# Attention and two feed-forward networks on one core: mirrored tiles turned one pair ahead, stores issued later, a subtraction on another engine

## The chip, the cores and the metric

One core of a Trainium2 chip runs the whole program in one launch. The metric is the device time of the execution in microseconds, as the median of several runs; lower is better.

## The reference

An attention without softmax (batch 2, sequence 3008, model width 256, key width 64) feeds two feed-forward networks in a row. All inputs are float32; the weights of the networks arrive as float64 words, which the kernel turns into float32 itself.

```python
scores = (1/S) * z @ z.T          # z: (2, 3008, 64), S = 3008
attn   = maximum(scores, 0) ** 2
x      = u * (attn @ v)           # u, v: (2, 3008, 256); x as (6016, 256)
h = x @ w_in1;  x = (h - tanh(h)) @ w_out1            # d_ff = 2048
h = x @ w_in2;  g = h where h >= 1, 0 where h <= -1, else (h + 1)**2 / 4
out = g @ w_out2
```

## The kernel before

Every float32 operand of a matmul is split into a rounded part and a rest (`hi`, `lo`), and three products replace one. ScalarE makes `hi` (a copy or a square with rounding), VectorE makes `lo` by a subtraction.

**Attention.** For each of two batches `b` there are six rows `c` of 512 queries (448 in the last), and in each row twelve pairs `t` of 128-key tiles, 144 pairs in all. A loop over the pairs (`i`, L1089) emits, for each: loads (`pump`), `get`s of mirrored blocks, hooks, the first product of pair `i` (`first_product`), the second product (with V) of pair `i - 2` (`second`, LAG = 2), a slice of weight conversion (`make`), and last the functions in `tail` (`close`). Each engine works its queue in this order; waits are on semaphores.

The score matrix is symmetric. A block of rows `c` and columns `e` with `c < e` is computed in row `c`, squared into `ax` and stored by `put` (L292) in a DRAM tensor `mir`; in row `e` it is fetched by `get` (L309) as two tiles `m` (eight DMAs, issued some pairs ahead), and `mirrored` (L324) turns its 32x32 blocks on VectorE into `am` (L333, two transposes), rounds it on ScalarE (`hi`, L337) and puts the subtraction (`lo`, L339) into `tail`. 60 of the 144 pairs are mirrored: none in row 0, two more in each further row, ten of twelve in row 5, so there they stand one behind the other. A pair that is not mirrored runs six score matmuls (L353), then relu and squares (L378, L381, L384) and `lo` (L396).

The queries of rows 0 to 4 are read by the score matmuls in a permuted order of 32-element runs (`turned`, L284), so the accumulators are permuted, and the end of a row undoes it (`y`, L457 on ScalarE and L458 on VectorE, read from PSUM; the next row's accumulation needs those banks). For the mirrored tiles to come out in that same order, `put` permutes rows while it stores, with four DMAs a tile.

**The queue of SyncE.** Nearly every DMA is issued from SyncE in program order: loads of z, v, u (L131, L136, L163, L268), `put` (L300 to L305), `get` (L318), conversion loads and stores (L196, L245), the finished rows (L471). One that waits for its source holds back all behind it. `put` and the rows' stores stand in `deferred`, which is emptied (`flush`) within the next pair.

**Conversion.** `convert` (L192) turns sixteen pairs of weight tiles (1024 columns of `w_in`, 512 of `w_out` each) into float32 halves on VectorE, ends with sums on GpSimd (L232), the rounding on ScalarE (L236), and the subtraction on VectorE (L241), and stores them. `work` gives it VectorE time as a credit: 1.5 for each pair that is not mirrored in rows 1 to 5, 1.4 for each `fill` in the networks; every step is charged its stated cost, the subtraction 1.2 or 0.69.

**Networks.** After the attention 88 units of 42 matmuls and the last tile's own loop follow; weights are streamed from DRAM for each unit.

Of the kernel before, what the change touches and what calls it, by code (L numbers as in the profile page):

```python
# [7 lines left out]
F32 = mybir.dt.float32  # L8
# [7 lines left out]
P = 128  # L16
# [15 lines left out]
def attention_then_two_ffn(  # L32
# [57 lines left out]

    loads = []
    deferred = []

    def add_load(first, last, steps, slots=1):
        loads.append({"first": first, "last": last, "steps": steps, "slots": slots})
# [3 lines left out]
            fn()  # L99
        deferred.clear()  # L100

    def split(hi, lo, src, now=False, on_vector=False):
        if on_vector:
            nc.vector.tensor_copy(out=hi, in_=src)
        else:
            nc.scalar.activation(out=hi, in_=src, func=AF.Copy)

        def rest():
            nc.vector.tensor_tensor(out=lo, in0=src, in1=hi.bitcast(F32), op=ALU.subtract)

        if now:
            rest()
        else:
            deferred.append(rest)
# [40 lines left out]
    def load_v(b, t):  # L155

        st = {}

        def dma(queue=nc.sync):
            r = st["raw"] = raw_p.tile([P, 512], F32, tag="raw", name=f"vraw{b}_{t}")  # L160
            r3 = r.rearrange("p (t d) -> p t d", d=D)
            n = min(2, NFULL - 2 * t)
            queue.dma_start(  # L163
                out=r3[:, :n, :],
                in_=v[b, 2 * t * P : (2 * t + n) * P, :].rearrange("(t p) d -> p t d", p=P),
            )
            if n < 2:
                for h in range(2):
                    nc.sync.dma_start(out=r3[64 * h : 64 * h + 64, 1, :], in_=v[b, NFULL * P :, :])

        def work(on_vector=False):
            r = st["raw"]
            w = ring.tile([P, 2, 512], F32R, tag="w", name=f"v{b}_{t}")
            if 2 * t + 1 < NFULL:
                split(w[:, 0, :], w[:, 1, :], r, on_vector=on_vector)
            else:
                split(w[:, 0, :D], w[:, 1, :D], r[:, :D])
                nc.scalar.activation(out=w[0:64, 0, D:], in_=r[0:64, D:], func=AF.Copy)
                split(w[64:128, 1, D:], w[64:128, 0, D:], r[64:128, D:])
            vs[b, t] = w  # L180

        return [(dma, AHEAD), (work, 2)]
# [9 lines left out]
    def convert(net, f, which, src):  # L192
# [45 lines left out]
        def rest():  # L238
            hi = st["hi"]
            lo = prep_p.tile([P, 1024], F32R, tag="lo", name=f"pl{nm}")  # L240
            nc.vector.tensor_tensor(out=lo[:, :n], in0=w[:, :n], in1=hi[:, :n].bitcast(F32), op=ALU.subtract)  # L241
            to = packed[net, f]
            for i, part in enumerate((hi, lo)):
                out_ = to[:, i, :] if which == "in" else to[:, 2, i * 512 : i * 512 + 512]
                nc.sync.dma_start(out=out_, in_=part[:, :n].bitcast(F32))  # L245
            done.add((net, f, which))

        if which == "in":
            posts.append((0.0, sums))
        posts.append((0.0, rounded))  # L250
        posts.append((1.2 if which == "in" else 0.69, rest))
        yield 0.69


# [37 lines left out]
    def put(b, c, t, a):  # L292

        e, h = divmod(t, 2)
        to = mir[b, c, e]
        tiles = slice(2 * h, 2 * h + 2)
        if e < QC - 1:
            to = to.rearrange("t p q -> (t p) q").rearrange("(i t b) q -> i t b q", i=4, t=4)
            for i in range(4):
                nc.sync.dma_start(out=to[i, tiles].rearrange("t b q -> b t q"), in_=a[32 * i : 32 * i + 32])  # L300
        elif t < NPA - 1:
            nc.sync.dma_start(out=to[tiles].rearrange("t p q -> p t q"), in_=a)
        else:
            nc.sync.dma_start(out=to[2], in_=a[:, 0])
            nc.sync.dma_start(out=to[3, :REST], in_=a[:REST, 1])  # L305
# [15 lines left out]
                )  # L321
            got[b, c, e].append((m, k))

    def mirrored(b, c, t):  # L324

        n = min(QT, S - QT * c)
        e, h = divmod(t, 2)
        a = tmp_p.tile([P, 2, 512], F32, tag="t2", name="am")
        hi = sp_p.tile([P, 2, 512], F32R, tag="hi", name="hi")
        lo = sp_p.tile([P, 2, 512], F32R, tag="lo", name="lo")  # L330
        s = (slice(None), slice(None), slice(0, n))
        for part, (m, k) in enumerate(got[b, e, c]):
            nc.vector.transpose(  # L333
                out=a[:, :, 256 * part : 256 * part + 32 * k].rearrange("p t (k a) -> p t k a", a=32),
                in_=m[:, :k, 2 * h : 2 * h + 2].rearrange("p k t a -> p t k a"),
            )
        nc.scalar.activation(out=hi[s], in_=a[s], func=AF.Copy)  # L337
        flush()
        tail.append(lambda: nc.vector.tensor_tensor(out=lo[s], in0=a[s], in1=hi.bitcast(F32)[s], op=ALU.subtract))  # L339
        return hi, lo, n  # L340

    def attn_s(b, c, t):
# [49 lines left out]
            tail.append(square_hi) if late else square_hi()  # L392
        flush()
        if out_:
            deferred.append(lambda: put(b, c, t, a))
        tail.append(lambda: nc.vector.tensor_tensor(out=lo[s], in0=a[s], in1=hi.bitcast(F32)[s], op=ALU.subtract))  # L396
        return hi, lo, n

    def attn_av(b, c, t, hi, lo, n):
# [7 lines left out]
        def mm(d, j, part, g, start=False, stop=False):  # L407
            for h in range(2):
                half = slice(64 * h, 64 * h + 64)
                lhsT = w[half, part, j * D + d * P : j * D + (d + 1) * P]  # L410
                nc.tensor.matmul(acc[d][h][:, :n], lhsT, g[half, j, :n], start=start, stop=stop)  # L411

        def his(d):
            for j in range(2):
# [45 lines left out]
        def scaled():  # L460
# [7 lines left out]
            while o < n:  # L468
                g, r = divmod(b * S + QT * c + o, 2 * QT)
                k = min(n - o, 2 * QT - r)  # L470
                nc.sync.dma_start(out=kept[0, g][:, :, r : r + k], in_=ut[:, :, o : o + k])  # L471
                o += k

        deferred.append(scaled)
# [93 lines left out]
    def fill():  # L568

        if fills:  # L570
            for fn in fills.pop(0):
                if fn is not None:
                    fn()
        else:
            work(CONVERT[1])

    def copy(out_, in_):
        nc.scalar.activation(out=out_, in_=in_, func=AF.Copy)  # L578
# [49 lines left out]
    class Unit:  # L628
# [59 lines left out]
        def emit(self, p, att=None):  # L688
# [60 lines left out]
            self.A.value()  # L749
            if att:  # L750
                flush()
            add(self.B.h[:, 0, :w], u2, V[:, :w])
            for fn in three:
                fn()
# [225 lines left out]
    with tc.manual_schedule():  # L980
# [88 lines left out]
                fn()  # L1069
            tail.clear()  # L1070

        def first_product(i):
            if i < len(pairs):
                s_fn, _, args = pairs[i]
                held[i] = s_fn(*args)
            else:
                flush()

# [7 lines left out]
        for k in range(3):  # L1086
            hook(NATT - 3 + k, load_w, k)

        for i in range(NATT):  # L1089
            pump(i)  # L1090
            while blocks and i + 1 >= blocks[0][3] - LEAD and sum(x > i for x in reading) < READ:
                *block, _, last = blocks.pop(0)
# [3 lines left out]
                fn(*args)  # L1096
            if i == LAG:
                second(i)
            if not (LAG < i - 1 and at[pairs[i - 1 - LAG][2]] == 0):
                first_product(i)  # L1100
            if LAG < i and at[pairs[i - LAG][2]] == 0:
                first_product(i + 1)
            if i == 0:
                close()
                z1["steps"][2][0]()
# [6 lines left out]
                second(i)  # L1112
            make(i)
            close()

        ps_s_guard.__exit__(None, None, None)
        ps_f = ctx.enter_context(
# [79 lines left out]
```

## Time and profile before

| | |
|---|---|
| median of 3 runs | 1520.16 us (1520.08 to 1520.57) |
| the profiled execution | 1520.33 us, span 1518.5 us |
| TensorE (matmul) busy | 1456.2 us, 96% of the span |
| VectorE busy | 1250.9 us, 82% |
| ScalarE busy | 981.1 us, 65% |
| GpSimd busy | 46.5 us, 3% |

The attention takes the first 545 us or so, the networks the rest. Engine names in the rows: PE is TensorE's matmul, PEld its weight load, DVE VectorE, ACT ScalarE, POOL GpSimd, SPq the queue of SyncE; L337 is line 337 of the kernel. The text gives the granted clock as a share of the full 2.4 GHz.

### The profile page before, as it was taken

Reading aid. Unit: us, or ns where it says so; the run is one execution under the profiler, and the core shown is the slowest. Engines: PE = TensorE matmul, PEld = TensorE weight load, DVE = VectorE, ACT = ScalarE, POOL = GpSimd, SP = SyncE. Lnnn points to the kernel's source line nnn. Section 1 sums busy time; section 2 is a strip of 40 time slices with the busy share of each in tenths; the row PEclk is TensorE's granted clock in tenths of the full one; section 3 lists DMA queues with packets and bytes.
Section 4 is the critical chain, followed back from the end, with each engine's and each line's share of the span. In section 5 each row is a group of like instructions: output and inputs, shape, how many; then the busy total and the mean of one; then the engine's idle time right before and its main releaser. Section 6 shows DMA issues by size and latency. Waiting matters only on the chain.

```text
span 1518.5 us, 22103 instructions
## 1 busy us (share of the span) xinstructions
PE 1456.2 (96%) x8293; PEld 1196.1 (79%) x8293; DVE 1250.9 (82%) x1551; ACT 981.1 (65%) x1209; POOL 46.5 (3%) x69
## 2 busy tenths in 40 slices
PE   8899898999987899999999999999999999999998
PEld 6688677786765678888888888988887878888897
DVE  6788778777876778989898988888889898888775
ACT  6687643887754366676767766766666666666543
POOL 0100000000000000000000000000000000000000
PEclk9899999999999999999999999999999999999999
DMA  7698878489878654837475665656554545647361
GB/s 177 194 279 243 218 176 198 121 238 264 231 196 219 211 208 127 321 121 275 172 239 202 235 238 206 247 203 223 181 151 163 169 168 184 204 151 234 125 194 25
DMA packets 282652, 301.12 MB, mean 198 GB/s; under 512 B 136880, under 2 KB 204848, under 8 KB 282544
## 3 DMA queue, kind: packets, MB, share of 16 engines
q1 hardware_dynamic: 281344, 299.44, 63.5%
q8 instruction: 65, 1.06, 0.3%
q10 hardware_dynamic: 1200, 0.26, 0.1%
q14 instruction: 43, 0.35, 0.1%
HBM read 225.84 MB, written 73.79 MB: 197 GB/s over the span
## 4 chain that ended last, share of the span: by engine, by line
PE 65%; ACT 9%; DMA 8%; DVE 7%; SPq 7%; issue 4%; ACTq 0%; DVEq 0%; POOL 0%; POOLq 0%
PE acc L661 29%; PE m L642 25%; PE acc L411 5%; SPq L318 3%; DMA m<-mir 3%; PE h L830 3%; ACT r L378 2%; DVE am L333 2%; PE acc L866 1%; SPq L300 1%; ACT hi L337 1%; PE acc L887 1%; ACT ax L384 1%; SPq L268 1%; DMA wideout<-in_moe_w_out_dram 1%
## 5 line engine op out<-in xcount | busy, mean ns | idle before, releaser
L411 PE MATMUL acc<-hi,v 64*128 64x512 f32 (+1 forms) x2256 | 311.1, 401 | 47.5 <-ACT hi L337 21.0
L411 PEld LDWEIGHTS acc<-hi,v 64*128 64x128 f32 x2256 | 232.1, 191 | 104.9 <-ACT hi L337 34.1
L642 PE MATMUL m<-xht,w 128*128 128x512 f32 (+1 forms) x704 | 215.7, 388 | 0.0
L661 PE MATMUL acc<-ghb,w 128*128 128x512 f32 (+1 forms) x704 | 187.8, 388 | 0.0
L661 PE MATMUL acc<-gha,w 128*128 128x512 f32 (+1 forms) x704 | 173.4, 387 | 0.0
L411 PE MATMUL acc<-lo,v 64*128 64x512 f32 (+1 forms) x1104 | 165.5, 394 | 2.9 <-DVE lo L396 2.6
L337 ACT ACTIVATE hi<-am 128x1024 fp32r<-128x1024 f32 (+1 forms) x60 | 61.4, 1023 | 155.1 <-DVE am L333 136.9
L661 PEld LDWEIGHTS acc<-ghb,w 128*128 128x128 f32 x704 | 131.1, 188 | 28.4 <-ACT ghb L578 0.7
L661 PEld LDWEIGHTS acc<-gha,w 128*128 128x128 f32 x704 | 132.1, 188 | 26.6 <-ACT gha L578 0.4
L642 PEld LDWEIGHTS m<-xht,w 128*128 128x128 f32 x704 | 132.2, 188 | 25.4
L604 DVE TENSOR_TENSOR ta<-ha,ta 128x1024 f32<-128x1024 f32 (+1 forms) x88 | 107.0, 1215 | 39.3 <-ACT ta L601 28.8
L642 PE MATMUL m<-xlt,w 128*128 128x512 f32 (+1 forms) x352 | 137.6, 391 | 1.4 <-ACT m L578 0.8
L411 PEld LDWEIGHTS acc<-lo,v 64*128 64x128 f32 x1104 | 119.3, 191 | 22.6 <-DVE lo L396 4.4
L615 DVE TENSOR_TENSOR gla<-ta,gha 128x1024 fp32r<-128x1024 f32 (+1 forms) x88 | 106.7, 1213 | 33.4 <-ACT gha L578 32.4
L578 ACT ACTIVATE u<-m 128x512 f32<-128x512 f32 (+1 forms) x176 | 102.6, 583 | 35.2 <-PE m L642 33.9
L578 ACT ACTIVATE ghb<-tb 128x1024 fp32r<-128x1024 f32 (+1 forms) x88 | 92.7, 1053 | 47.9 <-DVE tb L604 47.0
L615 DVE TENSOR_TENSOR glb<-tb,ghb 128x1024 fp32r<-128x1024 f32 (+1 forms) x88 | 106.8, 1214 | 17.4 <-ACT ghb L578 16.8
L339 DVE TENSOR_TENSOR lo<-am,hi 128x1024 fp32r<-128x1024 f32 (+1 forms) x60 | 70.7, 1178 | 51.1 <-ACT hi L337 50.6
L604 DVE TENSOR_TENSOR tb<-hb,tb 128x1024 f32<-128x1024 f32 (+1 forms) x88 | 106.5, 1210 | 5.0 <-ACT tb L594 0.2
L642 PE MATMUL m<-xhb,w 128*128 128x512 f32 (+1 forms) x352 | 107.7, 387 | 0.0
L578 ACT ACTIVATE gha<-ta 128x1024 fp32r<-128x1024 f32 (+1 forms) x88 | 92.2, 1048 | 17.6 <-DVE ta L604 16.8
L661 PE MATMUL acc<-glb,w 128*128 128x512 f32 (+1 forms) x352 | 94.4, 388 | 0.0
(109 smaller groups left out, 2441.3 us busy)
## 6 DMA issues: line engine op xcount, KB each, us to landing
w<-packed SPq DMA_DIRECT2D x288, 512.0 KB, 6.4
m<-mir SPq DMA_DIRECT2D x200, 128.0 KB, 3.7
mir<-ax SPq DMA_DIRECT2D x170, 128.0 KB, 2.7
xr<-kept SPq DMA_DIRECT2D x20, 512.0 KB, 6.9
widein<-in_moe_w_in_dram SPq DMA_DIRECT2D x16, 512.0 KB, 5.9
wideout<-in_moe_w_out_dram SPq DMA_DIRECT2D x16, 512.0 KB, 5.8
packed<-phin SPq DMA_DIRECT2D x16, 512.0 KB, 3.9
packed<-plin SPq DMA_DIRECT2D x16, 512.0 KB, 4.1
```

Source lines behind the costliest of these rows:

```text
L318: nc.sync.dma_start(out=m[32 * i : 32 * i + 32, :k].rearrange("b k t a -> b k (t a)"), in_=to[:, 8 * h : 8 * h + k, 128 * i : 128 * i + 128],)
L333: nc.vector.transpose(out=a[:, :, 256 * part : 256 * part + 32 * k].rearrange("p t (k a) -> p t k a", a=32), in_=m[:, :k, 2 * h : 2 * h + ...
L337: nc.scalar.activation(out=hi[s], in_=a[s], func=AF.Copy)
L339: tail.append(lambda: nc.vector.tensor_tensor(out=lo[s], in0=a[s], in1=hi.bitcast(F32)[s], op=ALU.subtract))
L378: nc.scalar.activation(out=r[s], in_=ps[s], func=AF.Relu)
L411: nc.tensor.matmul(acc[d][h][:, :n], lhsT, g[half, j, :n], start=start, stop=stop)
L578: nc.scalar.activation(out=out_, in_=in_, func=AF.Copy)
L604: nc.vector.tensor_tensor(out=self.t[self.s], in0=self.h[self.s], in1=self.t[self.s], op=ALU.subtract if self.net == 0 else ALU.max,)
L615: nc.vector.tensor_tensor(out=self.lo[self.s], in0=self.t[self.s], in1=self.hi.bitcast(F32)[self.s], op=ALU.subtract)
L642: nc.tensor.matmul(bank[:, : self.w], self.win[wp][:, block, :], xop[self.net, self.s][x][xp], start=start and i == 0, stop=True, skip_gro ...
L661: nc.tensor.matmul(self.acc(d, n)[:, : self.w], self.wout[:, part, j, d * P : (d + 1) * P], g[:, at, : self.w], start=start, stop=stop,)
L830: nc.tensor.matmul(banks[j][:, :n], win[wp][:, 2 * k + j, :], x[:, k, :n], start=(k == 0 and i == 0), stop=(k == 1 and i == 2),)
```

## The change

1. `prepare(i + 1)` emits the two transposes of a mirrored pair (`turn_m`) one pair earlier, right behind the first product of the pair before it; `mirrored` then only rounds and subtracts. The rounding of a mirrored pair that stands second in its row (it happens in row 5) goes into `tail`.
2. Stores go into a list `later` and are issued by `due()`, which runs at the start of each pair, in each `fill` and twice at the first unit: `put` and the stores of converted weights after a count of 2, the finished rows after a count of 1.
3. `put` stores rows in natural order, one DMA a tile in place of four (for the last tile two, as before); in rows 1 to 4 the second product reads mirrored tiles through `turned` in its place.
4. The subtraction of converted weights runs on GpSimd and is charged nothing; so does that of v's tiles, but for the first four of batch 0 and the odd last tile of each batch.

```diff
+    later = []
-    def split(hi, lo, src, now=False, on_vector=False):
+    def split(hi, lo, src, now=False, on_vector=False, engine=nc.vector):
...
-            nc.vector.tensor_tensor(out=lo, in0=src, in1=hi.bitcast(F32), op=ALU.subtract)
+            engine.tensor_tensor(out=lo, in0=src, in1=hi.bitcast(F32), op=ALU.subtract)
...
-                split(w[:, 0, :], w[:, 1, :], r, on_vector=on_vector)
+                split(w[:, 0, :], w[:, 1, :], r, on_vector=on_vector, engine=nc.gpsimd if b or t > 3 else nc.vector)
...  # convert
-            nc.vector.tensor_tensor(out=lo[:, :n], in0=w[:, :n], in1=hi[:, :n].bitcast(F32), op=ALU.subtract)
+            nc.gpsimd.tensor_tensor(out=lo[:, :n], in0=w[:, :n], in1=hi[:, :n].bitcast(F32), op=ALU.subtract)
...
+            def store():
+                ...
+            later.append((2, store))
-        posts.append((1.2 if which == "in" else 0.69, rest))
+        posts.append((0.0, rest))
...  # put
-        if e < QC - 1:
-            to = to.rearrange("t p q -> (t p) q").rearrange("(i t b) q -> i t b q", i=4, t=4)
-            for i in range(4):
-                nc.sync.dma_start(out=to[i, tiles].rearrange("t b q -> b t q"), in_=a[32 * i : 32 * i + 32])
-        elif t < NPA - 1:
+        if t < NPA - 1:
             nc.sync.dma_start(out=to[tiles].rearrange("t p q -> p t q"), in_=a)
...  # mirrored
+    def turn_m(b, c, t):
+        a = ahead[b, c, t] = tmp_p.tile([P, 2, 512], F32, tag="t2", name="am")
+        ...  (the two transposes, as before)
...
-        nc.scalar.activation(out=hi[s], in_=a[s], func=AF.Copy)
+        def round_hi():
+            nc.scalar.activation(out=hi[s], in_=a[s], func=AF.Copy)
+        tail.append(round_hi) if at[b, c, t] == 1 else round_hi()
...
-            deferred.append(lambda: put(b, c, t, a))
+            later.append((2, lambda: put(b, c, t, a)))
...  # attn_av
+                moving = g[half, j, :n]
+                if (t // 2, c) in MIRROR:
+                    moving = turned(moving, c)
...  # the finished rows
+                later.append((1, lambda to=to, src=src: nc.sync.dma_start(out=to, in_=src)))
...  # end of fill(); twice in Unit.emit at the first unit
+        due()
...
+        def prepare(i):
+            b, c, t = pairs[i][2]
+            if (t // 2, c) in MIRROR and (b, c, t) not in ahead and i not in held:
+                turn_m(b, c, t)
+        def first_product(i, both=False):
             if i < len(pairs):
                 s_fn, _, args = pairs[i]
+                prepare(i)
                 held[i] = s_fn(*args)
+                if i + 1 < len(pairs) and not both:
+                    prepare(i + 1)
...
+        def due():
+            now = [fn for k, fn in later if k <= 0]
+            later[:] = [(k - 1, fn) for k, fn in later if k > 0]
+            for fn in now:
+                fn()
         for i in range(NATT):
+            due()
             pump(i)
...
+            both = LAG < i and at[pairs[i - LAG][2]] == 0
...
-                first_product(i)
-            if LAG < i and at[pairs[i - LAG][2]] == 0:
-                first_product(i + 1)
+                first_product(i, both)
+            if both:
+                first_product(i + 1, True)
...
             make(i)
             close()
+            if both:
+                prepare(i + 2)
```

## Rows read from the trace of the kernel before

**Rows 1.** Windows by stage: window, its length, then busy (count) by engine, clock, DMA.

```profile
0.00:545.00 545.00, 489.74 (x3939) 393.93 (x3940) 419.05 (x554) 347.14 (x392) 25.19 (x41) 0.96 0.78 208
545.00:1518.50 973.50, 966.42 (x4356) 802.17 (x4354) 831.81 (x998) 633.92 (x818) 21.30 (x28) 1.00 0.56 193
...
230.00:273.00 43.00, 35.57 (x306) 30.83 (x306) 34.98 (x51) 20.36 (x27) 0.00 (x0) 0.92 0.69 163
```

**Rows 2.** What TensorE waited for: total us, times, longest us.

```profile
PE acc L411 <- ACT hi L337: 21.0, 23, 1.9
PE acc L411 <- ACT y L457: 14.3, 6, 5.0
PE acc L411 <- DVE v L109: 6.2, 2, 6.0
PE acc L411 <- DVE y L458: 5.2, 5, 2.7
```

**Rows 3.** Windows: an idle stretch; the stretch behind another. Columns as in rows 1.

```profile
229.80:233.70 3.90, 0.00 (x0) 0.00 (x0) 2.36 (x4) 1.45 (x3) 0.00 (x0) 0.76 0.97 240
...
493.20:498.00 4.80, 4.71 (x23) 4.11 (x25) 4.73 (x7) 1.66 (x4) 0.00 (x0) 0.50 0.00 0
```

**Rows 4.** Timeline, TensorE, an undisturbed stretch: start, us, engine line, shapes.

```profile
285.14 1.07 PE L353 MATMUL sc<-z,z 64*128 64x512 f32 x6
285.84 2.22 PE L411 MATMUL acc<-hi,v 64*128 64x512 f32 x16
...
288.60 1.07 PE L353 MATMUL sc<-z,z 64*128 64x512 f32 x6
```

**Rows 5.** Timeline of two mirrored pairs in row, VectorE and ScalarE [idle before].

```profile
471.45 1.30 DVE L333 STREAM_TRANSPOSE am<-m 128x512 f32<-128x512 f32 x2
472.84 1.06 ACT L337 ACTIVATE hi<-am 128x1024 fp32r<-128x1024 f32 x1 [2.56 <-DVE am L333]
473.93 1.23 DVE L339 TENSOR_TENSOR lo<-am,hi 128x1024 fp32r<-128x1024 f32 x1 [1.18 <-ACT hi L337]
475.07 1.30 DVE L333 STREAM_TRANSPOSE am<-m 128x512 f32<-128x512 f32 x2
```

**Rows 6.** Timeline, SyncE's queue, row 0.

```profile
20.61 1.94 SPq L300 DMA_DIRECT2D mir<-ax  x4
...
37.02 0.48 SPq L136 DMA_DIRECT2D zraw<-in_z_dram  x1
```

**Rows 7.** Timeline, VectorE, the waits for DMAs in rows 0 and 1.

```profile
39.30 0.71 DVE L142 STREAM_TRANSPOSE zt<-zraw 128x512 f32<-128x512 f32 x1 [6.21 <-DMA zraw<-in_z_dram]
...
61.66 0.43 DVE L203 TENSOR_SCALAR ein<-widein 128x512 uint32<-128x512 uint32 x1 [4.89 <-DMA widein<-in_moe_w_in_dram]
```

**Rows 8.** Timeline, SyncE's queue, the second of those loads.

```profile
57.03 0.58 SPq L196 DMA_DIRECT2D widein<-in_moe_w_in_dram  x1
```

**Rows 9.** Timeline, ScalarE, start of row 5 of batch 1.

```profile
491.80 0.95 ACT L337 ACTIVATE hi<-am 128x896 fp32r<-128x896 f32 x1 [2.90 <-DVE am L333]
492.66 1.07 ACT L457 ACTIVATE y<-acc 128x512 f32<-128x512 f32 x2
```

**Rows 10.** Groups by line: shapes, count, busy us, mean ns, idle before.

```profile
L333 DVE STREAM_TRANSPOSE am<-m 128x512 f32<-128x512 f32 x120 | 74.9, 663 | 0.0
...
L109 DVE TENSOR_TENSOR v<-vraw,v 128x512 fp32r<-128x512 f32 (+2 forms) x26 | 16.4, 637 | 0.1
```

**Rows 11.** Timeline: the closest fetch of a block, and its first use.

```profile
250.36 3.90 SPq L318 DMA_DIRECT2D m<-mir  x8
...
260.18 1.13 DVE L333 STREAM_TRANSPOSE am<-m 128x512 f32<-128x512 f32 x2
```

**Rows 12.** DMA issues: count, size, median us from issue to landing.

```profile
m<-mir SPq DMA_DIRECT2D x200, 128.0 KB, 3.7
```

**Rows 13.** Line 232 on GpSimd (min/median/max ns), then VectorE beside it.

```profile
L232 POOL TENSOR_TENSOR win<-win x64: 450/512/1453, 69.7 to 960.8; 128x128 f32<-128x128 f32 x64
...
97.78 1.51 DVE L396 TENSOR_TENSOR lo<-ax,hi 128x1024 fp32r<-128x1024 f32 x1 [0.73 <-ACT ax L384]
```

More of the change, by code (lines that the diff above doesn't have):

```diff
@@ L240, in rest @@
             lo = prep_p.tile([P, 1024], F32R, tag="lo", name=f"pl{nm}")
-            nc.vector.tensor_tensor(out=lo[:, :n], in0=w[:, :n], in1=hi[:, :n].bitcast(F32), op=ALU.subtract)
+            nc.gpsimd.tensor_tensor(out=lo[:, :n], in0=w[:, :n], in1=hi[:, :n].bitcast(F32), op=ALU.subtract)
             to = packed[net, f]
[L243 to L246, printed above, removed]
+            def store():
+                for i, part in enumerate((hi, lo)):
+                    out_ = to[:, i, :] if which == "in" else to[:, 2, i * 512 : i * 512 + 512]
+                    nc.sync.dma_start(out=out_, in_=part[:, :n].bitcast(F32))
+                done.add((net, f, which))
+            later.append((2, store))
         if which == "in":
@@ L322, in get @@
             got[b, c, e].append((m, k))
-    def mirrored(b, c, t):
-        n = min(QT, S - QT * c)
+    ahead = {}
+    def turn_m(b, c, t):
         e, h = divmod(t, 2)
[L328 to L331, printed above, removed]
+        a = ahead[b, c, t] = tmp_p.tile([P, 2, 512], F32, tag="t2", name="am")
         for part, (m, k) in enumerate(got[b, e, c]):
@@ L336, in mirrored @@
             )
-        nc.scalar.activation(out=hi[s], in_=a[s], func=AF.Copy)
+    def mirrored(b, c, t):
+        n = min(QT, S - QT * c)
+        a = ahead.pop((b, c, t))
+        hi = sp_p.tile([P, 2, 512], F32R, tag="hi", name="hi")
+        lo = sp_p.tile([P, 2, 512], F32R, tag="lo", name="lo")
+        s = (slice(None), slice(None), slice(0, n))
+        def round_hi():
+            nc.scalar.activation(out=hi[s], in_=a[s], func=AF.Copy)
+        tail.append(round_hi) if at[b, c, t] == 1 else round_hi()
         flush()
@@ L410, in mm @@
                 lhsT = w[half, part, j * D + d * P : j * D + (d + 1) * P]
-                nc.tensor.matmul(acc[d][h][:, :n], lhsT, g[half, j, :n], start=start, stop=stop)
+                moving = g[half, j, :n]
+                if (t // 2, c) in MIRROR:
+                    moving = turned(moving, c)
+                nc.tensor.matmul(acc[d][h][:, :n], lhsT, moving, start=start, stop=stop)
         def his(d):
@@ L470, in scaled @@
                 k = min(n - o, 2 * QT - r)
-                nc.sync.dma_start(out=kept[0, g][:, :, r : r + k], in_=ut[:, :, o : o + k])
+                to, src = kept[0, g][:, :, r : r + k], ut[:, :, o : o + k]
+                later.append((1, lambda to=to, src=src: nc.sync.dma_start(out=to, in_=src)))
                 o += k
@@ L751, in emit @@
                 flush()
+                due()
+                due()
             add(self.B.h[:, 0, :w], u2, V[:, :w])
@@ L1070, in close @@
             tail.clear()
-        def first_product(i):
+        def prepare(i):
[3 more added lines that the diff above has]
+        def first_product(i, both=False):
             if i < len(pairs):
                 s_fn, _, args = pairs[i]
+                prepare(i)
                 held[i] = s_fn(*args)
+                if i + 1 < len(pairs) and not both:
+                    prepare(i + 1)
             else:
@@ L1087, in attention_then_two_ffn @@
             hook(NATT - 3 + k, load_w, k)
+        def due():
[3 more added lines that the diff above has]
+                fn()
         for i in range(NATT):
+            due()
             pump(i)
```

## The prediction

> **What bounds the kernel now.** First I split the span by stage [rows 1]. In the networks TensorE is busy 966 of 973 us and its clock is full: nothing outside TensorE's own work can shorten them, and VectorE reaches 85% there without costing TensorE anything. What can be won lies in the attention: TensorE is busy 490 of 545 us at a mean clock of 0.96, so some 55 us are idle, and 545 x 0.04 = 22 us are lost to half clock. VectorE is busy for 419 of the 545, ScalarE for 347: neither is full on average, but in row 5 VectorE is at 35 of 43 us, where TensorE has the least to do.
>
> The second view is what TensorE waited for [rows 2]: the rounding of mirrored tiles (21.0 us, 23 waits), the ends of rows (14.3 and 5.2), and one tile of v (6.2). The third is the clock behind such waits [rows 3]: in one stretch TensorE does nothing for 3.9 us, and behind another it runs at 0.50, the lower of its two levels (1.2 GHz), for 4.8 us, which costs half of that. So a long wait costs more than its length.
>
> What the attention would take with no wait is read from an undisturbed stretch [rows 4]: six score matmuls take 0.70 us (285.84 - 285.14), the 24 of the second product 2.76 (288.60 - 285.84). 110 pairs of full width at 2.76, 22 of 448 columns at 2.76 x 448/512 = 2.42, the twelve last pairs of rows with 18 matmuls (2.07 or 1.81) and 84 x 0.70 for scores make 440 us, 3888 of the 3939 matmuls. The 13 of the warm-up and 38 of the networks (at 973/4356 = 0.22) and the first loads take some 17 more: 457 of 545 us. So 88 us is the most that can be won.
>
> **Turns one pair ahead.** Two mirrored pairs in row show the cause of the 21.0 us [rows 5]. VectorE turns (1.30), ScalarE rounds (1.06), VectorE waits 1.18 for it and subtracts (1.23); only then come the next turns, 3.62 us after the first. TensorE needs 2.76, in row 5 2.42: the pairs run at the pace of a round trip. With the next pair's turns in front of the subtraction, VectorE works while ScalarE rounds, the wait goes, and its share of a pair is 1.30 + 1.23 = 2.53, below 2.76 and about row 5's 2.42. Of 21.0 I take 18; the bounds are 10 (row 5 stays at VectorE's pace) and 21. The turns move past the weight conversion and the subtraction of one pair, which start 1.30 later; the second product reads that subtraction two pairs on, so about 4 us cover it. Without the cover it would cost 1.30 a pair.
>
> The turns now want their block one pair earlier. They have never waited for it: idle before 0.0 in 120 [rows 10]. The closest block is issued until 254.26 and first turned at 260.18 [rows 11], 5.9 us later; the flight takes 3.7 [rows 12], so 2.2 are left, and a pair of 2.5 to 3.6 earlier is 0.3 to 1.4 too much. In the other rows the fetch runs far ahead, so I count 0, at worst 1 us in each of ten blocks of row 5.
>
> **Rounding behind the end of the row.** In row 5 the first mirrored rounding stands on ScalarE in front of `y`: it waits 2.90 for the turns, and `y` comes at 492.66 [rows 9], while TensorE waits for the banks, 5.0 us at this place [rows 2] and 3.9 in the other batch [rows 3]. Put into `tail`, `y` passes it. The two waits make 8.9, their half clock about 2.4 each: 13.7. TensorE then has one pair of work before it needs that rounding, so I leave 1 us in each: 12. The other ends of rows (14.3 + 5.2 less 8.9 and the 2.7 below: 7.9) are partly queues of plain work on ScalarE and VectorE: I take 3, between 0 and 7.9.
>
> **Stores and SyncE's queue.** In row 0 a `put` issues four DMAs in 1.94 us [rows 6], 0.49 each; one saves 1.45. The whole queue there is issue after issue without a pause: z's last piece is issued at 37.02 [rows 6], VectorE stands 6.21 us at its transpose [rows 7], and behind it stands the subtraction of v for which TensorE waits up to 6.0 [rows 2]. Four puts before that issue save 5.8, and two more move behind it (3.9): it would go out some 9 us earlier. The 6.2 us go, with about 3 of half clock: of 9.2 I take 8.5, at least 5. In row 1 the first conversion issues its load at 57.03 [rows 8], and VectorE stands from 56.77 to 61.66 [rows 7]; `y` is behind it and TensorE waits 2.7 of the 5.2 [rows 2]. The load stands behind stores of fresh tiles; with those two pairs (about 7 us) later it should land in time. With the clock 5.7: I take 4, between 0 and 5.7. In all other rows a store that waits for its source still holds the queue, but two pairs of loads now go ahead of it: no gain counted, and for the tiles `ax` that wait longer, no loss, since SyncE, with three of four of their issues gone, can run ahead of the engines. If it did not, ScalarE would wait some 3 us a pair for a free tile.
>
> **Natural order.** 40 mirrored pairs in rows 1 to 4 (960 matmuls) now read through `turned`. The score matmuls of the same rows do so already: 0.70/6 = 0.117 us against 2.76/24 = 0.115 [rows 4]. Between 0 and 1.9 us; I take 0, as the difference is within the rounding.
>
> **GpSimd.** Eighteen subtractions of v (0.64 each, [rows 10]) leave VectorE: 11.5 us. The weights' leave it too, but their credit (1.2 and 0.69) is spent on the next conversion steps: 57 pairs x 1.5 = 85.5 pay for 85.5/7.5 = 11.4 pairs of weight tiles in the attention, where they paid for 85.5/9.4 = 9.1. So VectorE's load from weights stays and the conversion ends earlier, which the networks, bound by TensorE, can't use. What it costs: GpSimd's 128-column subtractions take 0.51, but up to 1.45 beside VectorE, and a VectorE subtraction took 1.51 there instead of 1.23 [rows 13, 5]. So the two hold each other up, by 0.28 for a short one. The new ones are four and eight times as long. Bounds for VectorE: 0.28 x 40 operations = 11 us, no more than leaves it; or the same share (0.28/0.51) of 18 x 2.05 + 11 x 2.05 + 11 x 4.1 = 104 us: 57. I take 20, nearer the measured case because GpSimd itself waited 0.94 where VectorE came first. About a third of the attention (rows 4 and 5) has no room on VectorE: 7 us on TensorE's path, between 0 and 19. In the networks some nine such operations fall on VectorE's 15% of room: 0, at most 5.
>
> The Trainium skill ("SBUF — State Buffer", section "SBUF: two separate sides") speaks against this move: a VectorE operation with two SBUF inputs and a GpSimd operation that reads SBUF exclude each other for a whole instruction. The row of 1.51 agrees. By the times in its "GPSIMD Engine Reference" (section 3.1, 4.50 us for 2048 columns) the new operations would hold VectorE for an estimated 57 us if each met one in full, 46 more than leaves it; a third of that makes 15 in place of my 7, and the sum 1487.
>
> **The sum.** 18 + 12 + 3 + 8.5 + 4 = 45.5; shorter waits (1 to 2 us) also drop the clock, of the 22 us some 11 are in none of these terms, and I take 3: 48.5. Less 7: 41.5. The profiled execution took 1520.33 (span 1518.5 and 1.8 around it): 1478.8. The median is 0.17 below it, so 1479.
>
> **The rivals.**
> *Half of it.* VectorE becomes the bound where the round trip was: in row 5 it has 35 of 43 us of work [rows 1], which neither the order of its queue nor GpSimd shrinks by more than 3. Then the mirrored term gives 10, the row ends 8, the loads 8, and GpSimd takes 8 back: 1502. For it: row 5's 35 us against 30 of TensorE. Against: 18 more us of waits are not throughput. Chance 0.17 (1495 to 1516).
> *Nearly all.* All waits go and GpSimd costs nothing: 88 less some 28 of start-up and row ends, 1460. Chance 0.09 (below 1465).
> *No change.* The stalls only move, for instance to fetches that are now late: 48.5 given back by ten blocks in row 5 would need 4.9 us each, against 1.4 at the closest [rows 11, 12]. Chance 0.03.
> *Slower.* GpSimd holds VectorE at the wrong moments: a long operation in front of a subtraction that TensorE needs next makes it wait, and the clock falls behind. From 48.5/40 = 1.2 us of TensorE's time for each operation on, the kernel loses. At 57 us on VectorE, all of it on the path, and 15 of half clock, it is 1520.3 - 48.5 + 72 = 1544. For it: [rows 13]; against: VectorE has 126 us of idle time in the attention. Chance 0.08.
>
> **How the numbers follow.** The forecast (1465 to 1495) has 0.63. A change of 0.2%, 3 us, is about what a measurement tells from none. Faster: 0.63 + 0.17 + 0.09 = 0.89; same 0.03; slower 0.08. The range leaves out the slower case and the no-change one (0.11), the part of the half case above 1510 (0.05) and a third of the best one (0.03): from 1458 to 1510.
>
> **What would show it.** In the profile after: waits of TensorE for the rounding of mirrored tiles under 4 us, and VectorE's wait for that rounding near 0; no long wait for `y` in row 5; no VectorE wait for z in row 0; one store of about 0.5 us a tile; the second product still at 2.76 in rows 1 to 4; attention ended near 503; networks still at 973. The prediction is wrong if VectorE subtractions of 2 us and more stand beside GpSimd's in number, if the turns wait for DMAs, or if ScalarE waits for stores.

## The result

The changed kernel takes 1531.05 us (median of 4 runs, 1530.69 to 1533.62) against 1520.12 for the kernel before in the same comparison: a ratio of 1.0077 [1.0060, 1.0094], so about 11 us slower where 41 us faster was forecast. The profiled execution took 1533.62 us, with a span of 1531.8.

The windows split at the end of the attention show two results of opposite sign (columns as in [rows 1]; the last three lines are a stretch of the networks in the kernel after, TensorE's idle time inside it, and what follows that):

```profile
0.00:511.00 511.00, 476.81 (x3920) 387.63 (x3921) 432.49 (x543) 348.36 (x392) 106.95 (x89) 0.98 0.82 232
511.00:1531.80 1020.80, 983.52 (x4374) 813.24 (x4372) 822.08 (x959) 633.23 (x818) 34.23 (x30) 0.98 0.52 179
600.00:632.00 32.00, 20.04 (x72) 15.17 (x71) 17.16 (x23) 13.46 (x18) 1.27 (x1) 0.79 0.67 247
...
613.10:622.20 9.10, 0.04 (x1) 0.00 (x0) 0.42 (x1) 2.03 (x3) 0.76 (x1) 0.72 1.03 419
622.30:630.00 7.70, 6.21 (x14) 4.43 (x15) 6.65 (x7) 5.08 (x6) 0.41 (x1) 0.50 0.27 109
```

In the timeline the last matmul of the second product ends at 510.1 us, where it ended at 539.5: the attention wins 29 us. From there to the end of the span it takes 1021.7 us, where it took 979.0: the networks, in which nothing was to change, lose 43. Before, TensorE idled 7 us in them [rows 1]; now 37, and the clock fell from 1.00 to 0.98.

What TensorE waited for in the kernel after (total us, times, longest us) names other lines than [rows 2] did:

```profile
PE m L658 <- ACT hb L594: 16.4, 2, 9.1
PE acc L425 <- ACT y L471: 10.2, 7, 3.3
PE m L658 <- ACT u L594: 8.2, 3, 3.3
PE m L658 <- ACT m L594: 5.5, 4, 1.5
PE acc L425 <- DVE y L472: 5.3, 8, 1.2
PE acc L425 <- ACT hi L346: 4.1, 2, 3.9
```

The wait for mirrored rounding (L337 before, L346 now) has fallen from 21.0 to 4.1, and the 6.2 for v are gone. New are 30 us of waits of the networks' matmuls (L658) for ScalarE's copies out of PSUM (L594). ScalarE itself waits in front of them:

```profile
ACT phout L237 <- DMA packed<-phin: 62.0, 12, 12.7
...
ACT phin L237 <- DMA packed<-phout: 12.2, 4, 4.6
```

That is the rounding of weights, and what it waits for is a store: the one that empties the rounded weights' buffer. Before, such waits came to 2.3 and 2.2 us.

One such wait, followed through four engines. First SyncE's queue (start, us, engine, line, DMAs), then ScalarE, then TensorE, all of the kernel after:

```profile
602.32 2.11 SPq L793 DMA_DIRECT2D kept<-y  x4
604.53 1.97 SPq L513 DMA_DIRECT2D w<-packed  x3
606.54 0.44 SPq L197 DMA_DIRECT2D wideout<-in_moe_w_out_dram  x1
607.08 2.32 SPq L513 DMA_DIRECT2D w<-packed  x3
609.44 0.44 SPq L248 DMA_DIRECT2D packed<-phin  x1
610.23 0.36 SPq L248 DMA_DIRECT2D packed<-plin  x1
```

```profile
595.50 1.05 ACT L237 ACTIVATE phin<-win 128x1024 fp32r<-128x1024 f32 x1
...
606.83 0.60 ACT L594 ACTIVATE u<-m 128x512 f32<-128x512 f32 x1 [0.26 <-PE m L658]
620.17 0.63 ACT L237 ACTIVATE phout<-wout 128x512 fp32r<-128x512 f32 x1 [12.74 <-DMA packed<-phin]
620.71 1.04 ACT L610 ACTIVATE ta<-ha 128x1024 f32<-128x1024 f32 x1
621.65 0.58 ACT L594 ACTIVATE hb<-m 128x512 f32<-128x512 f32 x1
```

```profile
612.52 0.61 PE L658 MATMUL m<-xhb,w 128*128 128x512 f32 x2
622.28 0.79 PE L658 MATMUL m<-xlt,w 128*128 128x512 f32 x1 [9.15 <-ACT hb L594]
```

Read it backwards. TensorE stands 9.15 us for a bank that the copy into `hb` has to empty. That copy is ready but stands on ScalarE behind the rounding `phout`. The rounding has one buffer, which still holds `phin`, rounded at 595.50. Its store was put into `later` and was issued at 609.44, 13 us after the rounding ended. For the first half of that time SyncE's queue stood, until 602.3, on a store of the networks' finished rows (L793) that waits for ScalarE's copy `y`. It is the longest of six such waits, 15.2 us:

```profile
SPq L793 <- ACT y L594: 86.9, 6, 15.2
```

Then those rows, streamed weights (L513) and raw weights (L197) were issued first. So in this one instance the list is only a part of the delay: with stores at once (experiment 1) the same tile's store still goes out 10.2 us after its rounding, behind the same L793. Over all 32 tiles, however, the median time from the end of a rounding to the issue of its store is 7.7 us in the kernel after and under 0.2 in experiment 1. From issue to landing the store took 10.6 us here, in a window where all DMA engines were busy (1.03, 419 GB/s above); the median flight of these stores rose to 6.3 us from the 3.9 before. Then the clock follows: 0.50 from 622.3 to 630. The kernel before had TensorE busy all through the same times, at 1.00:

```profile
600.00:632.00 32.00, 32.00 (x143) 26.50 (x142) 29.61 (x39) 21.78 (x29) 2.88 (x4) 1.00 0.77 259
```

### The profile page after: what moved, and what is told of

Same layout as the page of the kernel before. It is cut to its first block, busy times and chain, and to the rows that moved or that the text cites. A ratio compares the mean times of both kernels' runs of the same rounds, so it can differ in the third digit from the quotient of the medians.

```text
span 1531.8 us, 22008 instructions
## 1 busy us (share of the span) xinstructions
PE 1460.3 (95%) x8293; PEld 1200.9 (78%) x8293; DVE 1254.6 (82%) x1501; ACT 981.6 (64%) x1209; POOL 141.2 (9%) x119
## 4 chain that ended last, share of the span: by engine, by line
PE 65%; DVE 11%; DMA 9%; ACT 8%; issue 3%; SPq 2%; POOL 0%; DVEq 0%; ACTq 0%
PE acc L677 27%; PE m L658 23%; PE acc L425 9%; DMA packed<-phin 5%; PE h L848 3%; DMA m<-mir 2%; ACT r L389 2%; DVE lo L407 2%; PE acc L884 1%; PE acc L905 1%; DVE am L332 1%; ACT hi L392 1%; DMA packed<-phout 1%; ACT ax L395 1%; PE sc L364 1%
## 5 line engine op out<-in xcount | busy, mean ns | idle before, releaser
L425 PE MATMUL acc<-hi,v 64*128 64x512 f32 (+1 forms) x2256 | 309.6, 395 | 20.6 <-ACT y L471 10.2
L658 PE MATMUL m<-xht,w 128*128 128x512 f32 (+1 forms) x704 | 218.3, 392 | 0.0
L677 PE MATMUL acc<-gha,w 128*128 128x512 f32 (+1 forms) x704 | 176.6, 393 | 0.0
L425 PE MATMUL acc<-lo,v 64*128 64x512 f32 (+1 forms) x1104 | 168.6, 393 | 6.7 <-DVE lo L407 4.0
L658 PE MATMUL m<-xlt,w 128*128 128x512 f32 (+1 forms) x352 | 140.2, 398 | 30.7 <-ACT hb L594 16.4
L658 PEld LDWEIGHTS m<-xht,w 128*128 128x128 f32 x704 | 134.1, 190 | 25.3
L594 ACT ACTIVATE u<-m 128x512 f32<-128x512 f32 (+1 forms) x176 | 102.6, 583 | 38.8 <-PE m L658 37.6
L594 ACT ACTIVATE ghb<-tb 128x1024 fp32r<-128x1024 f32 (+1 forms) x88 | 92.6, 1053 | 49.8 <-DVE tb L620 49.7
L407 DVE TENSOR_TENSOR lo<-ax,hi 128x1024 fp32r<-128x1024 f32 x60 | 88.4, 1476 | 29.7 <-ACT ax L395 28.5
L594 ACT ACTIVATE gha<-ta 128x1024 fp32r<-128x1024 f32 (+1 forms) x88 | 92.3, 1048 | 27.4 <-DVE ta L620 25.9
L658 PEld LDWEIGHTS m<-xlt,w 128*128 128x128 f32 x352 | 66.8, 190 | 52.5 <-ACT hb L594 17.3
L658 PE MATMUL m<-xhb,w 128*128 128x512 f32 (+1 forms) x352 | 107.7, 387 | 0.0
L346 ACT ACTIVATE hi<-am 128x1024 fp32r<-128x1024 f32 (+1 forms) x60 | 61.2, 1022 | 69.3 <-DVE am L332 62.1
```

Of the source, the lines that this page charges most:

```text
L425: nc.tensor.matmul(acc[d][h][:, :n], lhsT, moving, start=start, stop=stop)
L658: nc.tensor.matmul(bank[:, : self.w], self.win[wp][:, block, :], xop[self.net, self.s][x][xp], start=start and i == 0, stop=True, skip_gro ...
L677: nc.tensor.matmul(self.acc(d, n)[:, : self.w], self.wout[:, part, j, d * P : (d + 1) * P], g[:, at, : self.w], start=start, stop=stop,)
```

## The experiments

Three causes could each explain it: the **late store** of weights that holds a single buffer; the **charge of nothing**, which lets the same credit start more conversion; and **GpSimd** in VectorE's way. The change ties all three to the conversion, so they are taken apart one by one; gains and losses below are ratios times 1520 us, and where a run is split into attention and networks, the times are those of its profiled execution (kernel before: attention to 539.5, networks 979.0; after: 510.1 and 1021.7). Diffs against the kernel after unless said otherwise. Eight results lie outside every range that was expected of them (experiments 2, 10, 11, and both runs of 6 and 7, the first of 8): several expectations let one cause act alone where two act.

**1. Stores of weights at once.**
```diff
-            later.append((2, store))
+            store()
```


> Changed kernel, but the stores of converted weights are issued at once, not two turns later. Theory A (the late store keeps the only buffer of rounded weights, and the next rounding blocks ScalarE): ScalarE's 62 us of waits for these stores nearly go, the networks (1016 us behind 516 in the changed kernel) return to about 975, the attention gains some more; 1475 to 1492 us. Theory B (GpSimd's subtraction holds VectorE up, and that costs the 42 us in the networks): still 1520 or more, since GpSimd's work is the same.

1487.42 us, 0.979 [0.9767, 0.9814]: the late store costs 44 us of the changed kernel. ScalarE's wait for stores falls from 74.2 (62.0 + 12.2) to 14.3 us, but the networks still take 998.7 us, 20 more than before, and this stays:

```profile
PE m L658 <- ACT hb L594: 7.1, 2, 4.2
```

So the late store is the largest part, and not all. The longest of these waits, 4.2, is at the place followed above: issued at once, the store stood behind L793 there.

**2. Two buffers, store as late as ever.** The rest `lo` is written over the source tile, which leaves room for two rounded ones.
```diff
-    prep_p = ctx.enter_context(tc.tile_pool(name="prep", bufs=1))
+    prep_p = ctx.enter_context(tc.tile_pool(name="prep", bufs=2))
-            lo = prep_p.tile([P, 1024], F32R, tag="lo", name=f"pl{nm}")
+            lo = w.bitcast(F32R)
```


> Changed kernel, but rounded weights have two buffers (their rests are written over the float32 weights, so the room is the same); stores stay two turns late, GpSimd subtracts. Theory A: the wait goes without an earlier store; 1475 to 1492 us. Theory B: still 1520 or more.

1498.81 us, 0.9856 [0.9832, 0.988]: 34 of the 44 us without touching the time of the store. The second buffer wins 30 us in the networks (991.3) and only 4 in the attention (506.2), where the early store won 23 and 24 (998.7 and 486.0). The wait has moved, as the source tile now waits for the store, and it is VectorE that does the waiting:

```profile
DVE win L221 <- DMA packed<-win: 22.6, 6, 7.0
...
DVE wout L221 <- DMA packed<-wout: 17.0, 6, 4.5
```

**3. The weights' subtraction back on VectorE.**
```diff
-            nc.gpsimd.tensor_tensor(out=lo[:, :n], in0=w[:, :n], in1=hi[:, :n].bitcast(F32), op=ALU.subtract)
+            nc.vector.tensor_tensor(out=lo[:, :n], in0=w[:, :n], in1=hi[:, :n].bitcast(F32), op=ALU.subtract)
```


> Changed kernel, but the weights' subtraction is back on VectorE (still charged nothing, its store still two turns late, one buffer). Theory A: the long waits in the networks stay, 1520 to 1540 us. Theory B: the loss goes, 1480 to 1495 us.

1523.5 us, 1.0031 [1.0017, 1.0046]: still slower than before, with the same signature (ScalarE behind stores, TensorE behind the copy):

```profile
ACT phout L237 <- DMA packed<-phin: 56.4, 12, 12.5
...
PE m L658 <- ACT hb L594: 15.9, 2, 8.8
```

GpSimd is 7 us of the changed kernel's time, and not the cause of these waits.

**4. The turns alone,** in the kernel before: `turn_m`, `prepare` and `round_hi` in `tail`, nothing else.

> Kernel before with the turns one pair ahead (and the rounding of row 5's second pair behind the end of the row) as the only edit. My prediction's terms for these two: 18 + 12 us, so 1490 us, and TensorE's wait for the mirrored rounding from 21 to under 4 us. Rival (the loads and SyncE's queue set the pace, so the wait only moves): 1512 to 1522.

1483.74 us, 0.9757 [0.9736, 0.9777]: 37 us faster. Two mirrored pairs in row, on VectorE and then on TensorE, against [rows 5]:

```profile
441.53 1.30 DVE L331 STREAM_TRANSPOSE am<-m 128x512 f32<-128x512 f32 x2
442.75 1.19 DVE L349 TENSOR_TENSOR lo<-am,hi 128x1024 fp32r<-128x1024 f32 x1
443.97 1.31 DVE L331 STREAM_TRANSPOSE am<-m 128x512 f32<-128x512 f32 x2
```

```profile
441.10 2.20 PE L421 MATMUL acc<-hi,v 64*128 64x512 f32 x16
...
443.82 2.20 PE L421 MATMUL acc<-hi,v 64*128 64x512 f32 x16
```

The next turns start 2.44 us after the first, not 3.62, VectorE's wait in front of the subtraction is gone here (over the run 3.0 us are left of 50.6), and TensorE runs a pair in 2.72. No wait for the mirrored rounding is left in its table; for the mirrored subtraction it now waits 6.3 us, before 0.2.

**5. The stores of the attention alone,** in the kernel before: natural order with one DMA a tile, the turned read, and `later` for `put` and the finished rows; weights as they were.

> Kernel before with natural order (one store a tile, second product through the permuted read) and late stores of tiles and finished rows as its only edits. My terms: 8.5 + 4 us, so 1507 (1500 to 1512), VectorE's 6.2 us wait for z in row 0 gone, matmuls of the second product as fast as before. Rival (the queue's relief is eaten by waits for free tiles or the slower permuted read): 1517 to 1525.

1501.15 us, 0.9881 [0.9866, 0.9896]: 18 us faster. SyncE's queue in row 0, against [rows 6]:

```profile
18.27 0.44 SPq L299 DMA_DIRECT2D mir<-ax  x1
...
31.03 1.42 SPq L137 DMA_DIRECT2D zraw<-in_z_dram  x1
```

A tile costs 0.44 instead of 1.94, and the last piece of z is issued at 31.03 instead of at 37.02. TensorE's wait for v falls from 6.2 [rows 2] to 0.9. What one DMA a tile and the later issue give each was not taken apart. Together experiments 4 and 5 give 55 us: the turns and the stores of the attention win at least what was forecast.

**6. The change without its weights' edits:** stores at once, charges of 1.2 and 0.69 again, VectorE again (v's subtraction stays on GpSimd). **And the same with the weights' subtraction on GpSimd.**
```diff
-            later.append((2, store))
+            store()
-        posts.append((0.0, rest))
+        posts.append((1.2 if which == "in" else 0.69, rest))
```


> Changed kernel without any of its edits to the weights (stores at once, charged, on VectorE); turns ahead, late stores of tiles and rows, one store a tile and v's subtraction on GpSimd stay. Theory A2: like the same with GpSimd within 4 us, 1463 to 1472. Theory B2: 1463 to 1470, 15 to 20 us below the same with GpSimd.

> Changed kernel, weights' stores issued at once and the subtraction charged 1.2 or 0.69 again; it stays on GpSimd. With stores at once alone the networks still took some 999 us against 979 before. Theory A2 (uncharged steps bring the next rounding so soon that the store of the last one hasn't landed): the networks return to about 979, in all 1463 to 1472 us. Theory B2 (GpSimd's subtraction costs them those 20 us): 1480 to 1490.

Without any of them 1458.15 us, 0.9605 [0.9589, 0.9621]: the attention ends at 477.7, the networks take 977.6. With GpSimd 1462.03 us, 0.9626 [0.9611, 0.964]; the intervals overlap a little. The first one's windows (the second window is cut off by the end of the span, at 1455.3):

```profile
0.00:478.00 478.00, 463.73 (x3918) 390.52 (x3919) 413.80 (x529) 345.67 (x387) 55.22 (x59) 0.99 0.85 237
478.00:1600.00 1122.00, 970.16 (x4377) 806.42 (x4375) 835.78 (x1004) 637.44 (x824) 21.32 (x28) 1.00 0.49 167
```

TensorE is busy 464 of 478 us in the attention, at 0.99. The three edits of the weights together cost 1531.05 - 1458.15 = 73 us: 32 in the attention (510.1 - 477.7) and 44 in the networks (1021.7 - 977.6), less what the execution profiled differs from the median.

**7. The charge, in both surroundings.** After, with stores at once, VectorE, and a charge of 0; and the kernel before with nothing changed but the charge:
```diff
-        posts.append((1.2 if which == "in" else 0.69, rest))
+        posts.append((0.0, rest))
```


> Changed kernel, weights' stores at once, subtraction on VectorE but charged nothing. Theory A2: the networks still lose 10 to 20 us, 1477 to 1492. Theory B2: 1465 to 1472.

> Kernel before with one edit: the weights' subtraction is charged nothing; it stays on VectorE, its stores are issued at once. Theory A2 (the charge was also the distance between a rounding and the next one on the same buffer): 1535 to 1550 us, with long ScalarE waits for the stores of rounded weights, in the networks above all. Rival (the charge is only bookkeeping of VectorE's time): 1515 to 1523.

1502.08 us, 0.9889 [0.9874, 0.9904], 43 us above experiment 6; and 1559.28 us, 1.026 [1.0242, 1.0277], 40 us above the kernel before. One number in an accounting line, with the same instructions in another order, costs 40 us: some 26 in the attention, which ends at 565.2, and 15 in the networks, which take 994.3. In the kernel before with that line, VectorE and ScalarE wait thus:

```profile
DVE ein L203 <- DMA widein<-in_moe_w_in_dram: 19.2, 5, 7.2
```

```profile
ACT phout L236 <- DMA packed<-phin: 22.0, 5, 7.5
```

The first is the raw weights, which are not there yet, all in the attention; the second the buffer again, though stores go at once, and 14.1 of it are in the networks. They were 4.9 and 2.3 in the kernel before: conversion now asks faster than the loads and stores deliver.

**8. Which of the two is it: pace, or buffer?** In the kernel before, the two buffers of experiment 2 beside the charge of 0; and charges kept, but a credit of a quarter more:
```diff
-CONVERT = 1.5, 1.4
+CONVERT = 1.88, 1.75
```


> Kernel before, uncharged subtraction, but two buffers for rounded weights. Uncharged with one buffer it was 1559. If the 40 us are waits for the one buffer: 1520 to 1532. If they are the faster pace itself (more conversion steps in each pair on VectorE, loads of raw weights too late for them): 1545 to 1560.

> Kernel before, charges kept, but the credit raised from 1.5 and 1.4 to 1.88 and 1.75, so that conversion goes at the pace of the uncharged kernel (9.39/7.5 = 1.25). If the pace makes the loss: 1545 to 1560. If the missing distance behind a subtraction makes it: 1518 to 1530.

1541.35 us, 1.0147 [1.0131, 1.0162]: the buffer explains 17 of the 40 us, most of them in the networks, which are back at 979.3, while the attention still ends at 561.1. 1548.89 us, 1.0199 [1.0184, 1.0214]: pace alone, with each step charged, costs 30, all of it in the attention (570.0; networks 980.5). In this last one ScalarE waits only 5.7 us for stores, but VectorE stands before raw weights of both kinds, and TensorE behind VectorE:

```profile
DVE eout L203 <- DMA wideout<-in_moe_w_out_dram: 16.7, 3, 7.8
DVE ein L203 <- DMA widein<-in_moe_w_in_dram: 16.0, 6, 4.2
```

```profile
PE acc L411 <- ACT hi L337: 29.6, 26, 4.1
...
PE acc L411 <- DVE lo L396: 14.7, 9, 4.8
```

So the credit kept conversion behind its own transfers. But a faster pace also moves work into the attention: VectorE is busy for 434 us of it here, before for 414. How much of the 30 us is this work and how much the waits for raw weights, these runs don't separate.

**9. How late.** The weights' store one turn late, with the charge of 0 and with the charges restored:
```diff
-            later.append((2, store))
+            later.append((1, store))
```


> Changed kernel with weights' stores one turn late in place of two (uncharged, GpSimd). At once it was 1487, two turns late 1531: if the wait grows with the delay, 1500 to 1522; if late is late, 1525 to 1535.

> Changed kernel with weights' stores one turn late in place of two, and the subtraction charged again (GpSimd). With stores at once it took 1462. If the late store alone holds the buffer too long: 1475 to 1500. If only uncharged work makes the wait: 1460 to 1466.

Uncharged 1517.23 us, 0.9991 [0.9978, 1.0005]: at once, one turn, two turns make 1487, 1517, 1531. Charged 1478.02 us, 0.973 [0.9716, 0.9745], 16 us above experiment 6 with GpSimd. So a late store costs about half as much when conversion keeps its pace (16 against 31), and the costs don't simply add. Two turns late with charges and one buffer, and the late store of weights alone in the kernel before, were not tried.

**10. Charges and two buffers, store two turns late.** Experiment 2 with the charges restored:

> Changed kernel with two buffers for rounded weights (rests written over the float32 weights) and the subtraction charged again; stores two turns late, GpSimd. With two buffers uncharged it was 1499; with one buffer, one turn late and charged 1478. If the single buffer is what makes a late store cost, 1458 to 1468; if late stores cost through something else (the float32 weights' own buffers, SyncE's order), 1475 to 1490.

1471.13 us, 0.9685 [0.9671, 0.97]: with charges and a second buffer, the store two turns late and GpSimd cost 12 us against the best of experiment 6. VectorE's wait for the source tile is down to 9.7 us from 22.6. The loss is all in the networks (992.4 against 977.6).

**11. GpSimd alone,** in the kernel before: only the weights' subtraction on it, charged as ever.

> Kernel before with one edit: the weights' subtraction on GpSimd, charged and stored as before. My prediction priced GpSimd at 0 to 19 us. From the two kernels with early charged stores (1462 on GpSimd, 1458 on VectorE): 1519 to 1526. If the lock on VectorE is cheap because waits absorb it: 1514 to 1519.

1528.89 us, 1.0064 [1.0047, 1.008]: 10 us slower, about 4 in the attention and 5 in the networks. TensorE's new wait is of the networks:

```profile
PE m L642 <- ACT m L578: 5.9, 8, 1.5
```

**12. The best version: experiment 6, and v's subtraction back on VectorE as well** (diff against the first run of experiment 6).
```diff
-                split(w[:, 0, :], w[:, 1, :], r, on_vector=on_vector, engine=nc.gpsimd if b or t > 3 else nc.vector)
+                split(w[:, 0, :], w[:, 1, :], r, on_vector=on_vector)
```


> The kernel without any edit to the weights (1458 us), and with v's subtraction back on VectorE too. My term for v: eighteen operations of 0.64 us, some of it won back by waits: 1456 to 1464. If GpSimd's lock costs more than it frees: 1450 to 1456.

1456.57 us, 0.9589 [0.9575, 0.9603], the lowest of all, and not to be told from experiment 6. It is the change without its fourth part and without the late stores of weights: 62 us faster than the kernel before and 74 faster than the kernel after.

## Why the prediction was wrong

**The step that failed** is the one on the weights, in the paragraph on GpSimd: that with the credit no longer charged "the conversion ends earlier, which the networks, bound by TensorE, can't use", with nothing on the networks but GpSimd's own "0, at most 5". The conversion does end earlier: its last operation on GpSimd starts at 808.2 us, before at 960.8 [rows 13]. But how soon it ends was not the point. What the networks lose is 43 us, from stalls on the way there; and the attention, though 29 us shorter than before, is 32 longer than without the edits of the weights (experiment 6). And the late store of weights got no term at all: the part on stores weighed `put` and the loads that pass it, and its "no loss" asked only whether `ax` has enough buffers. That the same list also held a tile with a single buffer, and that its next user stands on ScalarE in front of copies that TensorE needs, was open to read in the code; the test at the end of the prediction, "if ScalarE waits for stores", named the sign without the place.

Split at the end of the attention, the runs tell the two apart. The charge of 0 is what the attention pays for: in the changed kernel and its variants it ends between 474 and 479 us in the five runs with charges, between 486 and 510 in the six without; a late store adds to that only where the charge is 0, and VectorE is busy there for 408 to 414 us with charges and for 431 to 438 without. The single buffer is most of what the networks pay for: a second one gives them 30 us back in experiment 2 and 15 in experiment 8, and the attention 4 in each. With a late store and two buffers they still take 991 or 992 us, charged or not, against 978; the wait that makes this rest was not followed up.

From experiment 6 to the kernel after, one edit at a time: GpSimd +3, charge of 0 +25, one turn late +31, two turns +13, together 72. The order matters: without GpSimd the charge costs 43 (experiment 7) and with charges the first turn costs 16 (experiment 9). A split that holds in any order can't be given; that GpSimd softens the charge's cost is measured (25 with it, 43 without), why it does stays open.

**Turns and the rounding behind the row's end** were put at 18 + 12 = 30; alone they give 37 (experiment 4). Right in mechanism and somewhat small: the wait of 21.0 for the rounding goes entirely, that for the subtraction grows by 6, that for `y` on ScalarE falls from 14.3 to 7.0, and the mean clock of the attention is 0.98 instead of 0.96. Of the 7.0, one wait of 5.6 is at the start of row 5 of batch 1, where half of the 12 was counted: VectorE stands 7.51 us there for a load of the networks' input (`xr`), and ScalarE is idle for 6.43 in front of its own rounding of it, with `y` behind. The fetches, put at 0, were late: in experiment 4 seven times, 6.8 us of VectorE's time in all, in the kernel after twice, 2.9.

**SyncE's queue in rows 0 and 1,** 8.5 + 4 = 12.5: 18 (experiment 5). Right in mechanism. The issue of z came 6 us earlier, not 9, and VectorE still waits 2.97 for it in experiment 5; that was cover enough for v.

**Natural order** at 0, at most 1.9: the mirrored pairs of row 4, read turned, follow each other after 2.80 us (timeline below), the unturned ones of experiment 4 after 2.72. By 40 x 0.08 that is an estimate of 3.2, above the bound, which was worked out from other matmuls [rows 4]. Taking it out alone was not tried.

```profile
207.35 1.82 PE L425 MATMUL acc<-hi,v 64*128 64x512 f32 x14
...
210.15 1.82 PE L425 MATMUL acc<-hi,v 64*128 64x512 f32 x14
```

**GpSimd** at 7, between 0 and 19: 3 with stores at once and charges (experiment 6), 7 in the change as it stands (experiment 3), 10 alone in the kernel before; with stores at once and a charge of 0 the kernel is 15 us faster with it than without (experiments 1 and 7). Its operations were shorter than the price that I worked out from [rows 10, 13] (4.1 and 2.05 us):

```profile
L242 POOL TENSOR_TENSOR plin<-win,phin x16: 2357/2409/3382, 69.8 to 785.4; 128x1024 fp32r<-128x1024 f32 x16
L242 POOL TENSOR_TENSOR plout<-wout,phout x16: 1263/1286/2231, 80.8 to 808.2; 128x512 fp32r<-128x512 f32 x16
```

That the two engines hold each other up is there to see. GpSimd, then VectorE beside it:

```profile
92.39 2.41 POOL L242 TENSOR_TENSOR plin<-win,phin 128x1024 fp32r<-128x1024 f32 x1 [5.45 <-ACT phin L237]
```

```profile
92.46 2.63 DVE L206 TENSOR_SCALAR min<-widein 128x512 uint32<-128x512 uint32 x1
```

The second takes 0.42 us in the median and ends 0.29 after GpSimd's. The Trainium skill's rule that was weighed ("SBUF — State Buffer", section "SBUF: two separate sides") has one holder of a shared port for a whole instruction, and the trace agrees in that the wait lasts as long as GpSimd's operation. The prediction named the rule for VectorE operations with two inputs, and this one has one; the same rule of the skill names those in a "2-port perf mode" too, but no view here shows whether this one ran in it. The sum of 1487 that I had worked out by the rule took a term of 15 for GpSimd, 1.5 to 5 times what these runs showed.

**Clock and sum.** Without the weights' edits the change gives 60 us where 48.5 were summed: the sum holds to a quarter, and the two groups of terms that were run alone came out low. Of the 3 us put on the clock behind shorter waits no run shows the size; that the clock can fall behind them is in the kernel before, where waits of TensorE of 1.03 and 1.46 us end at 274.30 and 276.96 and the clock is 0.50 from 278 to 282, while behind one of 1.19 that ends at 482.43 it stayed at 1.00. The rival "nearly all" (1460) is what that version does. The rival "slower" came true in sign, by another mechanism than the one that was priced there.

## What to carry to other kernels

Before a store is put off, count the buffers of what it stores and ask who fills that buffer next and what stands behind it on that engine: one buffer and an in-order queue turn a store that nobody waits for into one that TensorE waits for. Ask also what the issuing queue itself will stand on at that time. An accounting of credit and charges that meters background work is a throttle on its transfers as well as on its engine; moving a step to an idle engine doesn't make it free to start sooner, so leave its charge in, or measure the new pace by itself. A change of several parts whose sum is wrong should be measured by halves: here the turns and the attention's stores won 60 us and the edits of the weights lost 72.

## What the runs showed that was not expected

A charge of 0 in place of 1.2 and 0.69, with the same instructions, made the kernel before 40 us slower (1.026 [1.0242, 1.0277]). GpSimd's subtraction of 1024 columns took 2.41 us and of 512 columns 1.29, against 0.51 for 128 [rows 13], so a longer one is far cheaper for each column. And an operation of VectorE with one input, of 0.42 us in the median, took 2.63 beside it.
